# A speech codec's end tiles: another order for the planner's steps, and 89 copies on the other engine

## Chip, cores and metric

The kernel runs on one NeuronCore of a Trainium2 chip. The metric is the time of one execution on the device in microseconds (us). The engines are named as in the profile: PE (TensorE, matrix products, its weight loads as PEld), DVE (VectorE), ACT (ScalarE), POOL (GpSimd) and SP (SyncE, which issues DMAs).

## What is computed

The input x has 2 sequences of 16,000 rows with 512 bf16 values. Each row goes through an encoder, four stages of a residual quantizer with 8 codewords each, and a decoder. The reference, cut:

```python
for i in range(K):                                   # K = 3 taps over rows
    z = z + xp[:, i:i+T, :] * dw_enc[i][None, None, :]
z = _silu(z)
res, q = z, jnp.zeros_like(z)
for s in range(Nq):                                  # 4 stages
    cb = codebooks[s]                                # 8 x 512
    d2 = |res|^2 - 2 res.cb + |cb|^2
    sel = cb[d2.argmin(-1)]
    q, res = q + sel, res - sel
for i in range(K):
    y = y + qp[:, i:i+T, :] * dw_dec[i][None, None, :]
```

The stages depend on each other, since each subtracts the codeword that the one before it chose.

## The kernel before

**Tiles.** Each sequence is cut into nine tiles. A tile has G rows on each of 128 partitions, G = 16 but for the two at the outer ends: the tiles are 4, 10, 16 x 7 and 16 x 7, 10, 4 rows, numbered 0 to 17. The end tiles of four and ten rows make the first and the last stretch of the kernel short.

**Steps of a tile.** The rows are loaded transposed (`XT`, L599, one DMA for each of the G rows, issued by SP). *Front*: for each half of the channels, six products with the taps (L644 on ACT, L645 on DVE), two sums on DVE (L393, `TA` and `ZB`), then exp on ACT (L650), plus one (L651 on ACT, L652 on DVE), reciprocal on ACT (L662), and the gate on DVE (L393, `ZB<-ZB,EX`). Exp and reciprocal lie in different tables, so a change from one to the other costs a table load. *Score*: PE forms products with the codebooks (L674, L681), DVE takes them out (L715, L716). *Decide*: three decisions with short DVE operations (L393, L742, L774); between them PE transposes the one-hot choice (L758), a copy of it (`OT`, L762 on ACT, L763 on DVE) goes back to PE for a correction (L768). The third decision writes `OHD`; PE transposes the one-hots (L791), a copy takes them out (`OHR`, L796, called "win0"). *Resid*: PE rebuilds the residual with the chosen codewords (L838, L843) in four units of 8 and 32 products, and 8 copies write it over `ZB` (L865 on ACT, L866 on DVE). *Score3* and *decide3* choose the fourth codeword on the residual (L881, L882, L890), PE transposes again (L808), a copy takes it out (`OHW`, L814, "win3"). *Back*: PE multiplies the one-hots with the decoder's table (L915, L917, L919), copies to `YB` (L924 on ACT, L925 on DVE), and stores by SP (L952).

**The order.** Nothing is issued at once. Every step is put on a list with its engine, its planned cost and what it depends on: 2408 steps. `Plan.order` then gives out the list. Two strings fix what it does: `RANK` holds two characters for each step, its place in its engine's queue, and `WHERE` holds a letter (A or D) for each of the 608 steps that may run on ACT or on DVE (`either`). Each engine takes its steps strictly by rank. The planner's clock decides only which PSUM bank a product gets and where **filling matmuls** (L973) go: products without a use that are put in front of a PE step when the planner believes that PE would stand idle, so that the granted clock stays up. On the chip each engine runs its queue in order and waits where an operand is not there.

**Buffers around the order.** The residual of tile n+4 shares a `ZB` buffer with tile n: the front of a later tile can write its `ZB` only when the last score of the earlier tile has read it. SP's queue holds loads and stores in one order.

Of the kernel before, what the change touches and what calls it, by code (L numbers as in the profile page):

```python
# [185 lines left out]
def kernel(  # L186
# [31 lines left out]
    NA = 4  # L218
    QUOTA = {"ACT": 4, "DVE": 4}
    DIGITS = "0123456789abcdefghijklmnopqrstuvwxyzABCDEFGHIJKLMNOPQRSTUVWXYZ"  # L220
    RANK = ("00010200010703060F0c070G0e0005010b0k0n0d0i0e0o090J0a0h0j000v03090j060e0405070f0i0u0k0o000D0l0x010202080a0b0e0f0j0k040609"
            "0c0d0g0h0i05060b01040a0407080305090g0l080d02030h0r0y0u0B0v0m0c0Q0V0W0Y1012130q0w0D0g0F0a0b0n0s1p1w1B1l1n1z0c0m0x1q1u1N0n"
            "0j0q0y080d0w0B0C0H0I0L0P0R0f0m0l0C0p0r0U0s0A0t0z0q0h181a1d0O0K0E0T0k1k0o1r0p1s0i1i0M0f0N0g0S0X0Z110p1m14171516191b1c1e0t"
            "0A0z1y0E1A0r1G1H1I1J1L1P1S0l0s0N0t1W1Y202322242627292a0m0u0Q0v2c2e2g2f2h2i2j2k0n0y2m0A0B0T0U0C0D2w2x0E0F0W0Y0G0H0Z0X0J2I"
            "2K2M2N2P0L110N150O3c151j1f1g1h1o1v1t1x0H0J1E0G1C1D1F0I1K1M0K1U0L1Z0O2d0w0z2n0x2o2q2r2s2t2u2v0o0I2B0K2y2z2E2G2H2J2L2O2Q2S"
            "0p0M2X0P2V2W2Y31333435370q0Q170R0S3e190T0U3f1a0V0W3j1e0X0Y1d1c11123q133r3t3u3w3x141i181p1a1q1u191l1b1m1F171k1r040a0b0l0i"
            "0j090c02070d0f08060k030h051T1O1Q1R1V0M1X210R2p252b280P2l0S0V2A102R1232143b0Z103s15163B3D3F3H3J3L3M0r1e3P1g3T3V3X3Z3U3W40"
            "4142430s1i1t1j4447494a4d4e4h4i0t1k4m1l1m1x1A1n1o4t1z1p1q1E1C1r1s1F4A1w1y4P1z1A4U4W4Z51531E1L1I1O23231Z1H1N1K1R1X1L1Q1Z25"
            "2b1G1M2224250A0t0B0z0g0v0o0n0p0m0r0w0x0u0s0q0e0y2T2F2C2D2Z133036181b3a1638393d3h3g3i1f3p1g3y1j3G1d1f3O1c1h3Y4b464g4l4o4s"
            "0u1u1G1x4w4B4D4K4G4H4M4O4Q4S0v1B1J1D4T4X50525456585a0A1J1P1M1N1T1U1O1P1V1W1Q1R1Y1X1U1V202120215J24255Q5S5V5Z6129682c2a2d"  # L230
            "2b2c2b292f2c2o2s2o2t6F2v2l6n2C2u2s0F0H0O0T0S0L0E0N0D0M0R0J0I0Q0C0K0G0P3k3n3l3m3o1h3v3z1n3R3C3K3E3A3N1o3Q3S1u4j1v4q1w4y1v"
            "1C4Y1t1F575d595f5i5k2U5m0w1X5A1Y5p5r5t5y5E5F5G5I5K5L0z2626275M5N5P5U5Y6264660B2a6a2e2g2f2e2h2i2g2h2j2m2j2l2p2q2n2m2y2z6T"
            "2A2F6X6Y74767a2O7j2Q2D2R2G2F2S2E2X7w2M2T2F312N2R2V2H302Q2P120Y0X1316191b181c0Z0U170W10140V111a1s45481r4c4k4f4n1y4z4p4u4r"
            "4v4x1D1B4C1H4N1I551K5c1S1W5D1T285X6560676c6j3I6m0D2n2k2r6o6q6s6t6u6v6x6y6z6A0F2v6D2x6C6E6G6H6I6K6L6O0H2B2r2E2G2w2v2I2J2y"
            "2B2K2M2A7i2N2Y7x2K33347G35377O7T7V7Y823g2U3t363u37343i2X3r34303o333s35383j2Z3p8l2V1j1s1o1v1k1e1t1g1d1m1p1f1l1n1h1q1w1i4F"
            "4J4E4I4L4R4V5b1S5o5e5h5j5g5l5q5n5s1Z5H225O276e2k2o6w2u2w6J6M6N6P6R6S6U0G2D2s2H6V70797c72787e7f7h7l0I2Z2J327r7t7z7C7D7F7H"
            "7J0K362O393a7Z2S3d3e2V2W3h3k32303v3w8E8F3A3E8J3I3L8X8Z9496983Q9c413s3X3u3s3T3l3U3n3k3W3t473y3z3V3m403p3B1B1A1O1x1D1C1G1J"
            "1I1K1H1N1E1L1z1y1M1P5x5w5v5u5z5B5C5R286g5W695T636b6d2d6f2i6p2p6Q2q6W2L2P7m2U2W7v7y7E7I7K7M7N0J382P3f7R7U7X81838587898f8h"
            "0L3m313q8j8m8p8o8r8u8w8x0N3x8C3y3z3b8G3C3D3d3c3F3H3e8S3J3K3f3h3O3P9b3R3S9f9h9n9q9s4a3A4f3G4m3M3N4g3H4l3K3L4n3L4u3O3M4w3R"
            "4q3V411U26281S291V221Y1Q231W1R1T272021240x0y6k6l6i6h6r2t6B6Z2z7p732x7571777d7b7g2C7u2I7B2L7L3b3c8g3l3n8k8t8s8y8z8A8B0M3B"  # L240
            "3a3G8D8H8K8M8L8N8P8Q8R8T0O3M3g3N8U8V92939597999e0P3Y3q44453x3w48499E3B4b4c3D3E4d4e9K3F4o4pad4i4jaeagaiakam4y3S4B3W4C3Y4g"
            "4A3U4P45464L424Z4a4c4V4b554e4h2n2u2j2k2p2h2t2e2d2a2l2g2i2q2r2f0C0E2m7k7n7o7q7s7A2M7P2T8e7S7W7Q2R808684882Y8q388O398I3Z42"
            "9y43469A9C9G9I9L9M9P0Q4h3I4k9R9U9W9Y9Xa0a2a4a5a60R4r3P4va8afajalanaparax0T4D3X4G4H40414N4O44aV4Q4R47b44S4Tb6484W4Ybl5154"
            "bqbubybCbE5e4k5h4o5m4t4B5n4r5z4B4A5K4I5J4K4F5B4C5G4H4D2J2z2w2B2G2L2A2Q2H2K2x2D2C2E2y2I2N2O8a8b8d8c8i8v8n8W3j9l8Y903i919a"
            "3k9d9g3r9t3v9B3z9H4s4tac4x4zatawavaBaDaGaI0S4KaO4MaKaMaPaYaRaXaZb0b3b50U4U494Xb7b9bbbabcbdbebf0W50bj52534d4c56584g4j5b5c"
            "4m4i5k5l4p4q5p5qc45x5ycicncrctcz5L4J5N4L5S4P4I5O4M5R4O4W5U4R5Z4U4S5Y4T604V4N392Z2X3b2T2Y2W333d2U35363a37313c2S329j9i9k3o"
            "9m9o9p9r3C9N9u9w9x9v9z9F9D9J3Ja33Nay3Qaq4F4JaL4E4IaNaTaUb1bgbhbi0V57bp59bkbmbnbvbtbwbAbDbHbI0X5g4l5ibLbQbRbObTbVbXbY105o"
            "c15r5s4uc85t5u4w4x5v5w4z4y5D5E4E4F5M5PcJ5I5QcLcOcQcVcY624W664Z6m594X6k5a6p5c4Z6q5e6w5g506idB6t5d523e3u3w3i3q3n3o3t3p3l3v"
            "3f3m3r3j3h3x3g9O9S9T9Q9V9Za1a73TaAa9abaaahaoasauaz3ZaJ43b246b85a5dbG5f5jbMbUbSc2c3c7c90Y5A4A5CcbcccdcfckcmcocqcvcB0Z5T4Q"
            "5WcGcIcNcTcWcZd1d31261d663644Yd9656750526869dh536c6e57566j6ndL6r6sdTdXdZe1e36ye96O5y6Zf1536E5m6I5p546Q5t6S5z556Keu6V5x56"  # L250
            "3S3I3C3K3U3D3y3R3H3O3G3Q3F3T3J3A3E3PaEaFaHaCaQaSaWbo4hbZbr4fbsbxbzbFbBbJ4nc64sce4vcg5F5Hcw5V5XcRcXcUd2dbdddf116adr6gdidk"
            "dpdtdvdxdAdCdEdF146ldH6odIdKdNdMdOdPdQdS156udV6v6x5k5h6z6A5jee6F6Geo5o6L6M5r5s6T6UeQ6W6YeZf0f5f7f978fg7c5I7vfM5a7j5M7g5N"
            "597ifB7nfD587ofE7p5P57473V4b404a4f3W453Z423Y434d3X49484e44bKbPbNbWc0c5cach4Dcycpclcscjcu4GcxcA4Nd74Sd84Xdg6b6ddo6f6hdudy"
            "dwdDdWe0e4166D5l6He7eaecejeqereteweyez186PeC6ReBeDeIeLeNeOePeR1b6XeW70715Cf87476fa5F777a5Hfn7b7dfq5K7k7lfC7u7zfUfVfYg0g1"
            "7D5U7K5X7M5Y5d7Igi7P5Z5b7G5W7Ogn5c7S6081655e4n4o4p4x4y4w4r4v4l4i4t4m4u4z4q4k4j4scCcDcFcEcHcKcMcP51dld5d4cSd0dadcdedj55dG"
            "58dR5be26B6Ceg6J6NeAeHeJeMeTeUeV1972f375eYfdfifjf6fffkflfmfo1a7e5J7hfpfrfuftfvfyfzfA1d7m5O7q7r5QfJ7s7w5R5S7y7Ag45T7C7F5V"
            "g77J7Ngm7U7YgAgCgDgIgK86gN8a698d6b5f8e6c8i6d5g8fgT8k6e5h8ggU8lgW5i4O4M4T4J4K4G4P4H4L4C4E4Qdndqdm54dsdJdzdU5iehe5e65fdYe8"
            "ebedef5nes5qeF5veX7379fc7ffsfwfxfFfGfHekfI1c7tfL7xfKfNfQfRfPfSfTfWfXfZ1e7Bg37Eg2g6g8g5g9gbgdgg1h7Lgk7Q7R61go7V7X63628083"
            "67668487gP688h8jgV8ogXgYgZh0h18rh38u6j8w6k5k8t6i8vh95j8yhb5l4V4R514U4Y1317eiemenelepevexeE5A5E5ueG5weKeS5Bf2f45Dfb5Gfh5L"
            "fO7Hgagegcgfghgjfegl1f7Tgs7Wgpgqgrgugtgvgwgxgygz1g7Z6482gBgFgGgEgHgJgLgM1i85gO8889gQgR8b8cgS6a8m8n6g6f8p8q6hh28sh4h5h6h7"  # L260
            "h88xha8z6l8A6m5m")
    WHERE = ("DADAAAAADAADDDDADADDDDDDDDDAAADAADDAAAAAADDDDDDDADADDADDDDADADADAAAAAAAAADDDDADDDDDAAADDADAADAAAADAAAAAAAAADDDDADADADDDD"
            "DAAAAAAAAAAADAAAAADDADDDDADDDDDDADDDADAAAAAAAADAAADAAAAADDADDDDDDDAADADAAAAAADDAAAAAAAAADDDDDDDDDDDDDDDAAADAAAAADDDAAAAA"
            "AAADDDDDDDDDDDDADAADADAAADAAAAAAAAAAADDDDADDDADDDDDAAAAADAAADAAAAAAAAAADDDDDADDDDADDDAAAAAADADDAAAAAAAAAADDDDDDDDDADADDD"
            "ADAAAAAAAAAAAAAAAAADDDADDDDDDDDDDDADADAAAAAAAAAAAAADADDDDDDDDDDDDDDAADADAADAAADADAAAADADDDDDDDDADDDDDDDDAAADDAAADADAADDD"
            "ADDDDDDDDDDDADDADDADDAADDAAAADAADAADDDDDDDDDDDDDDDAAADAADAADDAAAADADDDDDADDDDDADDDDDDDADAAAADADAAADDDDDDDDAADADADDDADDDD"
            "AAAADDAA")
    assert B == len(SIZES) and T >= GM * P and GM <= 16

# [83 lines left out]

    plan = Plan(NA, QUOTA, [len(DIGITS) * DIGITS.index(a) + DIGITS.index(b) for a, b in zip(RANK[::2], RANK[1::2])], WHERE)
    add = plan.add
# [655 lines left out]
```

## Time and profile before

| | us |
|---|---|
| three runs | 618.36, 619.06, 619.17 (median 619.06) |
| the profiled execution | 619.28 |
| its span, first to last instruction | 617.2 |
| mean granted clock of PE | 0.976 |
| filling matmuls L973 | 426, busy 106.5 |
| table loads | 36, 1.28 each |

In the profile a line such as `L924 ACT CAST YB<-banks ... x107 | 104.7, 1026 | 16.0 <-PE banks L915 11.8` reads: line, engine, operation, what is written from what, count; total busy us and mean ns of one; idle us of the engine just before them and who ended it. In a timeline the idle time stands in brackets behind the instruction that it precedes, with its releaser. In the chain each piece is start, length and what ran; it is followed back from the last instruction. In a table by stretches each engine has its busy us and, in brackets, its instructions; the last three numbers are the granted clock, the share of the DMA engines and GB/s. Records of neighbouring instructions on one engine overlap by some 0.08 us, so mean and busy time over count differ a little.

### The profile page before, as it was taken

What the parts mean: (1) busy time and instruction counts of PE and PEld (TensorE: products, weight loads), DVE (VectorE), ACT (ScalarE), POOL (GpSimd) and SP (SyncE); (2) the same over time, 40 slices, a digit from 0 to 9 for tenths busy, and PEclk for the clock granted to TensorE, in tenths of its full rate; (3) what the DMA queues carried; (4) which work ended last, traced back from release to release, by engine and by line L of the source; (5) the groups of instructions that cost most, each with busy time, mean ns of one, the idle gap of its engine ahead of it and who ended that gap; (6) DMA issues with size and microseconds to landing.
All of it is one profiled execution on the core that took longest, in us unless ns stands there. A gap on an engine that the chain in (4) does not pass through costs nothing.

```text
span 617.2 us, 27847 instructions
## 1 busy us (share of the span) xinstructions
PE 509.7 (83%) x12649; PEld 244.2 (40%) x12649; DVE 574.7 (93%) x1134; ACT 548.9 (89%) x428; POOL 48.1 (8%) x86
## 2 busy tenths in 40 slices
PE   4797978987877889877895965988988879899995
PEld 3344434433434334343342343444344333434452
DVE  5999999899999999999999999989999999998764
ACT  4899899799999999999969999969999999975563
POOL 1002000110010011011000010101000101000000
PEclk9889999999999999999999987899999999999999
DMA  7424437455637687475575576565646425043236
GB/s 215 95 53 95 83 87 108 82 98 116 107 79 140 125 127 162 87 133 115 126 144 107 118 146 167 115 143 113 89 111 157 128 63 149 4 139 139 83 102 208
DMA packets 155562, 71.84 MB, mean 116 GB/s; under 512 B 146886, under 2 KB 146918, under 8 KB 155316
## 3 DMA queue, kind: packets, MB, share of 16 engines
q1 hardware_dynamic: 155228, 69.64, 52.1%
q8 instruction: 98, 1.61, 1.1%
q10 hardware_dynamic: 216, 0.43, 0.2%
q14 instruction: 20, 0.16, 0.1%
HBM read 2.26 MB, written 32.77 MB: 57 GB/s over the span
## 4 chain that ended last, share of the span: by engine, by line
DVE 48%; PE 18%; ACT 12%; issue 9%; SPq 6%; DMA 5%; ACTq 0%; DVEq 0%
DVE ZB L393 10%; DVE TB L645 7%; DVE TA L393 6%; PE banks L838 5%; DVE TA L645 4%; SPq L599 4%; PE banks L915 3%; DMA XT<-in_x_dram 3%; PE banks L681 3%; PE banks L843 3%; DVE EX L652 3%; ACT TB L644 3%; ACT EX L650 2%; ACT YB L924 2%; ACT ZB L865 2%
## 5 line engine op out<-in xcount | busy, mean ns | idle before, releaser
L924 ACT CAST YB<-banks 128x1024 bf16<-128x1024 f32 x107 | 104.7, 1026 | 16.0 <-PE banks L915 11.8
L865 ACT CAST ZB<-banks 128x1024 bf16<-128x1024 f32 (+2 forms) x107 | 94.3, 925 | 26.1 <-PE banks L843 26.1
L650 ACT ACTIVATE EX<-ZB 128x4096 bf16<-128x4096 bf16 (+2 forms) x36 | 115.3, 3202 | 1.6 <-DVE ZB L393 1.2
L662 ACT ACTIVATE EX<-EX 128x4096 bf16<-128x4096 bf16 (+2 forms) x36 | 114.7, 3193 | 0.5 <-DVE EX L652 0.3
L973 PE MATMUL banks<-MSK,IDENT 128*128 128x512 bf16 x426 | 106.5, 392 | 3.5 <-issue 2.8
L681 PE MATMUL banks<-ZB 128*32 128x64 bf16 x8064 | 92.0, 198 | 5.3 <-DVE ZB L393 3.3
L681 PEld LDWEIGHTS <-ZB 128*32 128x32 bf16 x8064 | 77.3, 96 | 46.6 <-issue 38.7
L915 PE MATMUL banks<-WDEC,OHW 128*128 128x512 bf16 x252 | 73.6, 383 | 18.7 <-ACT ZB L865 4.4
L843 PE MATMUL banks<-OHR,WR 32*128 32x512 bf16 (+3 forms) x1152 | 82.1, 355 | 0.1
L645 DVE TENSOR_SCALAR TB<-XT,WENC 128x2048 bf16<-128x2048 bf16 (+2 forms) x120 | 80.2, 678 | 0.1
L393 DVE TENSOR_TENSOR ZB<-TA,TB 128x4096 bf16<-128x4096 bf16 (+2 forms) x36 | 72.6, 2017 | 5.3 <-PE banks L681 3.4
L838 PE MATMUL banks<-ZB,IDENT 64*64 64x512 bf16 (+3 forms) x576 | 54.9, 369 | 24.2 <-ACT ZB L865 7.2
L393 DVE TENSOR_TENSOR ZB<-ZB,EX 128x4096 bf16<-128x4096 bf16 (+2 forms) x36 | 72.8, 2024 | 1.1 <-ACT EX L662 1.0
L393 DVE TENSOR_TENSOR TA<-TA,TB 128x4096 bf16<-128x4096 bf16 (+2 forms) x36 | 72.5, 2014 | 0.4 <-ACT TB L644 0.3
L753 POOL COPY OHD<-OHA 128x256 bf16<-128x256 bf16 (+2 forms) x36 | 30.6, 850 | 479.5 <-DVE OHA L393 479.5
L973 PEld LDWEIGHTS <-IDENT 128*128 128x128 bf16 x426 | 39.7, 100 | 48.7 <-issue 10.4
L838 PE MATMUL banks<-ZB,UP 64*64 64x512 bf16 (+3 forms) x576 | 53.1, 353 | 0.3 <-issue 0.3
L843 PEld LDWEIGHTS <-WR 32*128 32x128 bf16 x1152 | 23.2, 92 | 59.0 <-issue 51.3
L644 ACT ACTIVATE TB<-XT,WENC 128x2048 bf16<-128x2048 bf16 (+2 forms) x24 | 42.3, 1763 | 2.8 <-DVE ZB L393 2.7
L866 DVE CAST ZB<-banks 128x1024 bf16<-128x1024 f32 (+3 forms) x37 | 38.2, 1042 | 7.0 <-PE banks L843 6.9
L645 DVE TENSOR_SCALAR TA<-XT,WENC 128x2048 bf16<-128x2048 bf16 (+2 forms) x65 | 44.1, 689 | 0.2
L838 PE MATMUL banks<-ZB,DOWN 64*64 64x512 bf16 (+3 forms) x576 | 42.0, 365 | 0.4 <-issue 0.4
(132 smaller groups left out, 602.0 us busy)
## 6 DMA issues: line engine op xcount, KB each, us to landing
out_dram<-YB SPq DMA_DIRECT2D x29, 512.0 KB
out_dram<-YB SPq DMA_DIRECT2D x32, 448.0 KB
XT<-in_x_dram SPq DMA_TRANSPOSE x267
out_dram<-YB SPq DMA_DIRECT2D x28, 60.0 KB
ZB<-in_x_dram SPq DMA_DIRECT2D x1, 1280.0 KB
ZB<-in_x_dram SPq DMA_DIRECT2D x1, 512.0 KB
out_dram<-YB SPq DMA_DIRECT2D x30, 2.0 KB
out_dram<-YB SPq DMA_DIRECT2D x2, 224.0 KB
```

What stands on the lines that cost most here:

```text
L393: add("DVE", cost, key, lambda: nc.vector.tensor_tensor(out=out, in0=a, in1=b, op=op), reads, writes, **kw)
L644: either({"ACT": act(R), "DVE": dve(R, 3.84) + 0.06}, key, lambda dst=dst, src=src, w=w: nc.scalar.mul(dst, src, w), lambda dst=dst, src=s ...
L645: lambda dst=dst, src=src, w=w: nc.vector.tensor_scalar(out=dst, in0=src, scalar1=w, scalar2=None, op0=ALU.mult),
L650: add("ACT", act(2 * R), ("exp", n, h), lambda: nc.scalar.activation(v(ex), Z, ACT.Exp, scale=-1.0), zt, [("EX", sl), "ACTTAB"], hold="E")
L662: nc.scalar.add_instruction(mybir.InstActivation(name=nc.get_next_instruction_name(), engine=mybir.EngineType.Activation, func=ACT.Reciprocal,
L681: nc.tensor.matmul(o[HB * q:HB * (q + 1), u * ZW:(u + 1) * ZW].rearrange("p (s c) -> p s c", s=2), lhsT=blk, rhs=both, start=False, stop=( ...
L838: nc.tensor.matmul(at(r)[to], lhsT=dia[h, h], rhs=Z[h, i, r:G:RG, :], start=start, stop=False)
L843: nc.tensor.matmul(at(r), lhsT=WR[v][g, i * P:(i + 1) * P], rhs=W[g, v // 3, 0:rows_of[r], :], start=False, stop=stop)
L865: either({"ACT": act_psum(2 * k * P), "DVE": dve(2 * k * P)}, key(1), lambda dst=dst, src=src: nc.scalar.copy(dst, src()), lambda dst=dst, ...
L915: nc.tensor.matmul(o, lhsT=W[:, k, PADC:PADC + P], rhs=WDEC[u], start=True, stop=not wrap)
L924: either({"ACT": act_psum(1024), "DVE": dve(1024)}, key, lambda dst=dst, box=box: nc.scalar.copy(dst, ps(box)), lambda dst=dst, box=box: n ...
L973: nc.tensor.matmul(PS[j // 2][:, 512 * (j % 2):512 * (j % 2) + NMK * ZW], lhsT=IDENT, rhs=MSK.rearrange("p u w -> p (u w)"), start=True, s ...
```

## The change

Only the two strings change. No step is added or removed, no cost, buffer or dependency is touched. All lines of `RANK` and all but the last of `WHERE` are new:

```diff
-    RANK = ("00010200010703060F0c070G0e0005010b0k0n0d0i0e0o090J0a0h0j000v03090j060e0405070f0i0u0k0o000D0l0x010202080a0b0e0f0j0k040609"
...
-            "h88xha8z6l8A6m5m")
-    WHERE = ("DADAAAAAADAADDDDADADDDDDDDDDAAADAADDAAAAAADDDDDDDADADDADDDDADADADAAAAAAAAADDDDADDDDDAAADDADAADAAAADAAAAAAAAADDDDADADADDDD"
...
+    RANK = ("00010200010c05080M0d070L0c000j0f0f0k0p0c0g0g0r090N0e0j0t000t050h0m080l0b0k090d070F010r000g0c0B020403040607090a0h0i010208"
...
+            "h38xh58z6q8A6r5m")
+    WHERE = ("DADAAAAADAADADDDADDDDDDDDDAAAADAAADAAAAAADDDDDDDADDDDADDADADADAADAAAAAAAADDDDADDDDDAAADAADAADAAAADDAAAAAAAADDDDADADADDDD"
...
             "AAAADDAA")
```

Read letter by letter against the list of steps, 89 of the 608 steps change engine:

| copies (columns) | ACT to DVE | DVE to ACT |
|---|---|---|
| taps of 16 rows (2048) | 1 (tile 10) | 3 (tiles 6, 9, 13) |
| taps of 10 rows (1280) | 3 | 1 |
| taps of 4 rows (512) | 4 | 3 |
| `OT` (128 and less) | 10 | 7 |
| "win0" `OHR` (1024) | 2 (tiles 8, 15) | 3 (tiles 10, 12, 14) |
| "win3" `OHW` (1024, one of 640) | 1 (tile 2) | 4 (tiles 3, 6, 12, 16) |
| residual (1024) | 10 | 10 |
| residual of end tiles (256 to 768) | 2 | 4 |
| `YB` (1024) | 9 | 11 |
| setup (`WR`, L536) | 0 | 1 |

The queues of PE (533 steps), POOL (81) and SP (333) keep their steps in another order: the longest run of steps that keep their order among themselves is 356, 56 and 131. ACT has 400 steps instead of 395 (253 in the old order), DVE 1061 instead of 1066 (568).

More of the change, by code (lines that the diff above doesn't have):

```diff
@@ L220 @@
     DIGITS = "0123456789abcdefghijklmnopqrstuvwxyzABCDEFGHIJKLMNOPQRSTUVWXYZ"
-    RANK = ("00010200010703060F0c070G0e0005010b0k0n0d0i0e0o090J0a0h0j000v03090j060e0405070f0i0u0k0o000D0l0x010202080a0b0e0f0j0k040609"
[L222 to L260, printed above, removed]
-            "h88xha8z6l8A6m5m")
@@ new lines @@
+    WHERE = ("DADAAAAADAADADDDADDDDDDDDDAAAADAAADAAAAAADDDDDDDADDDDADDADADADAADAAAAAAAADDDDADDDDDAAADAADAADAAAADDAAAAAAAADDDDADADADDDD"
+            "DAAAAAAAAAAAAAAAAADDADDDDADDDDDDADDDDDAAAAAAAADAAADAAAAADDADDDDDDDAADADAAAAAADDAAAAAAAAADDDDDDDDDDDDADDAAAAAAAADDDAAAAAA"
+            "AAADDDDDDDDDDDDADDADAAADAAAAAAAAAAAAADDDDADDDADDDDDDADAADAAAAAAAAAAAAAADDDDDADDDDAADDDAAAADDADAAAAADAAAAADDDDDDDDDADDDDD"
+            "DAAAAAAAAAAAAAAAAAADDDADDDDDDDDDDADDDDAAAAAAAAAAAAADADDDDDDDDDDDDDDDAAADAADAAAAADAAAADADDDDDADDADDDDDDADDAAAADDADAAADAAA"
+            "ADDDDDDDDDDDADDDAADADAADADAADAADAAADDDDDDDDDDDDDDDDDADAAADADDAADDADAADDDDADDDDDDDDDADDAAAADADAADDAAADDDDDDAADDADDDADDDDA"
```

44 lines of the change are left out of this document (39 added, 5 removed).

## Prediction, made before the run

> **What bounds the kernel now.** I read the page first, for the shares.
>
> ```profile
> span 617.2 us, 27847 instructions
> PE 509.7 (83%) x12649; PEld 244.2 (40%) x12649; DVE 574.7 (93%) x1134; ACT 548.9 (89%) x428; POOL 48.1 (8%) x86
> ```
>
> Three engines are above 80%, so a mean says little. I cut the span where the character of the 40 slices changes and asked for the busy time of each engine in three stretches.
>
> ```profile
> 15.00:415.00 400.00, 325.10 (x7693) 155.28 (x7694) 389.61 (x693) 373.42 (x268) 32.65 (x38) 0.97 0.58 114
> 415.00:541.00 126.00, 109.08 (x3067) 51.34 (x3052) 122.99 (x238) 125.17 (x94) 11.12 (x13) 1.00 0.44 101
> 541.00:611.00 70.00, 68.93 (x1854) 31.73 (x1846) 53.81 (x150) 43.10 (x51) 2.45 (x9) 1.00 0.37 130
> ```
>
> The columns are stretch, length, then PE, PEld, DVE, ACT and POOL busy. Up to 541 us DVE idles 10.4 of 400 and 3.0 of 126 us; ACT idles 26.6 and 0.8. So VectorE sets the pace, and from 415 on ScalarE is as full. In the last 70 us PE is busy for 68.9 and the other two are not. The waits of that last stretch (who waited for whom: total us, times, longest) say the same:
>
> ```profile
> ACT ZB L865 <- PE banks L843: 15.3, 11, 3.3
> ACT YB L924 <- PE banks L915: 8.1, 9, 1.5
> DVE ZB L866 <- PE banks L843: 6.6, 8, 1.9
> PE banks L838 <- issue: 0.3, 1, 0.3
> ```
>
> So the time is a sum: the moment at which the decisions of tile 14 are made, which lets PE start that tile's residual, then some 70 us of PE work, then the last copy and store. The hand-over, from the timelines of DVE, PE and ACT, and the end, from the chain:
>
> ```profile
> 537.84 0.28 DVE L393 TENSOR_TENSOR OHD<-KEY,M 128x128 bf16<-128x128 f32 x1
> 539.88 0.68 DVE L796 COPY OHR<-banks 128x1024 bf16<-128x1024 bf16 x1
> ```
>
> ```profile
> 540.60 0.41 PE L838 MATMUL banks<-ZB,IDENT 64*64 64x512 bf16 x4
> ```
>
> ```profile
> 610.37 1.01 ACT YB L924
> ```
>
> The last decision of tile 14 (OHD) ends at 538.12, the copy of its transposed rows (L796) at 540.56, the residual starts at 540.60, the last copies run from 610.37, and the span ends 6.8 us later. The profiled execution took 619.28 us, 2.1 more than its span and 0.2 more than the median of 619.06.
>
> One more thing costs time ahead of the hand-over: **PE trains**. When a tile's third decision is made, PE transposes it, runs four residual products and scores, and both other engines wait for it. From the chain:
>
> ```profile
> 298.95 0.29 DVE OHD L393
> ...
> 314.72 0.66 PE banks L681 x63
> ...
> 315.41 2.29 DVE ZB L393
> ...
> 410.68 0.30 DVE OHD L393
> ...
> 415.60 0.34 PE banks L681 x16
> ...
> 415.96 1.53 DVE ZB L393
> ```
>
> The reader is to see a DVE decision, PE alone, and DVE again: tile 7's train, 299 to 315, and tile 10's, 411 to 416.
>
> **The change part by part.** The 2408 steps are the same ones; the strings only say on which engine a copy runs and where each step stands in its engine's queue. I sorted every queue by the old and by the new ranks and added up, for each step, its duration in this trace (its time beyond the end of the instruction before it).
>
> *Moved copies.* 42 go from ACT to DVE and 47 back. The rates, total over count of these rows (groups by line and shape):
>
> ```profile
> L924 ACT CAST YB<-banks 128x1024 bf16<-128x1024 f32 x107 | 104.7, 1026 | 16.0 <-PE banks L915 11.8 <-PE banks L919 3.9
> L925 DVE CAST YB<-banks 128x1024 bf16<-128x1024 f32 x19 | 22.9, 1216 | 2.8 <-PE banks L915 1.3 <-PE banks L919 1.0 <-issue 0.6
> L644 ACT ACTIVATE TB<-XT,WENC 128x2048 bf16<-128x2048 bf16 x18 | 36.1, 2003 | 2.8 <-DVE ZB L393 2.7
> L645 DVE TENSOR_SCALAR TB<-XT,WENC 128x2048 bf16<-128x2048 bf16 x94 | 69.1, 744 | 0.1
> L814 ACT COPY OHW<-banks 128x1024 bf16<-128x1024 bf16 x8 | 8.2, 1023 | 0.3 <-PE banks L808 0.3
> L796 DVE COPY OHR<-banks 128x1024 bf16<-128x1024 bf16 x8 | 5.4, 680 | 0.0
> ```
>
> Net to ACT go 2 output copies (0.98 us there, 1.21 on DVE), 2 long taps (2.00 and 0.74) and 3 window copies (1.02 and 0.68): ACT +9.0, DVE -5.9. Net to DVE go 3 short taps (two of ten rows, by the long rate times 10/16, one of four rows, by 4/16): ACT -3.0, DVE +1.1. Ten residual copies of 1024 go each way. The rest, net 3 copies of 128 columns to DVE and 5 copies of the end tiles and the setup to ACT, I estimate from the same rates by width: ACT +0.5, DVE -0.7. In all **ACT +6.5, DVE -5.5 us**, over the whole kernel. Table loads stay 36: the order in which exponentials and reciprocals alternate has as many switches.
>
> *Work ahead of the hand-over.* That is what counts. Check of the method: the busy time up to 538.13, grouped, is
>
> ```profile
> 0.00:538.13 538.13, 438.20 (x10719) 210.95 (x10720) 518.34 (x979) 501.68 (x374) 45.29 (x76) 0.97 0.56 114
> ```
>
> and my old queue has 518.3 us of DVE work up to tile 14's decision. In the new one 27 copies worth 16.5 have left, 26 worth 15.0 have come, and a score copy of 0.5 stands behind: 516.4, so **-2.0**. The copy of the rows itself (L796) goes to ACT: +0.3 by the rates. On ACT 26 copies worth 18.9 have left ahead of it and 28 worth 23.6 have come, that copy among them: **+4.7**.
>
> *The train of tile 10.* DVE and ACT idle at it (timelines):
>
> ```profile
> 415.96 2.29 DVE L393 TENSOR_TENSOR ZB<-TA,TB 128x4096 bf16<-128x4096 bf16 x1 [2.20 <-PE banks L681]
> ```
>
> ```profile
> 409.61 1.93 ACT L924 CAST YB<-banks 128x1024 bf16<-128x1024 f32 x2 [2.15 <-PE banks L915]
> 414.94 1.93 ACT L865 CAST ZB<-banks 128x1024 bf16<-128x1024 f32 x2 [3.41 <-PE banks L843]
> 418.33 2.00 ACT L644 ACTIVATE TA<-XT,WENC 128x2048 bf16<-128x2048 bf16 x1 [0.55 <-DVE ZB L393]
> ```
>
> In the new queues decision 10 comes 5.9 us of DVE work earlier, the gate of tile 12 (2.2 us) stands between it and the waiting sum, and on PE the last score of tile 9, which that sum waits for, no longer stands behind the 2.2 us second half of tile 10's first residual product. I take the DVE wait from 2.2 to 0.3: **-1.9**; bounds: 0 (the train waits for ACT) and -2.2. Next late is ACT, which now also copies tile 10's rows.
>
> *ScalarE's way to that copy.* The hand-over is the later of two ways. DVE's stands at -2.0 + 0.3 - 1.9 = -3.6. ACT's is +4.7 less what ACT no longer idles. Between 415 and 541 it has 0.8 us to spare; before, 26.6. The three rows above hold 6.1 of these, and two rows at tile 7's train another 4.3:
>
> ```profile
> 311.19 1.01 ACT L865 CAST ZB<-banks 128x1024 bf16<-128x1024 f32 x1 [1.70 <-PE banks L843]
> 314.76 1.01 ACT L865 CAST ZB<-banks 128x1024 bf16<-128x1024 f32 x1 [2.56 <-PE banks L843]
> ```
>
> Decision 7 comes 3.8 us of DVE work earlier in the new queue, decision 10 5.9. I take the 6.1 and a quarter of the 4.3, 7.2 in all: ACT arrives at 4.7 - 7.2 = **-2.5**, later than DVE, and sets the hand-over. Bounds: +4.7 (nothing absorbed) and -3.6 (DVE's way).
>
> *The last 70 us.* PE has the same 99 steps, 69.3 us, from tile 14's residual to the end in both queues; DVE has 52.6 instead of 54.3 us left, ACT 44.4 instead of 42.6. I take **0**. Bounds: +2 (a dozen order changes among PE's steps, each waiting at most for one copy of 1 us), -1.7 if DVE's share set it.
>
> By the Trainium skill's page Perfetto Trace Analysis (Identifying the Most-Contended Engine), matmul busy time is no measure of how near PE is to its limit, weight loading is; weight loads fill 31.7 of the 70 us, so by that PE has room. The waits quoted above, ACT and DVE for PE and PE for neither, speak against it here. By its rule the last stretch would follow DVE: -1.7, a rival below.
>
> *At nothing.* Two rows of the chain, a burst of filling matmuls and a transposing load on the path:
>
> ```profile
> 105.98 3.73 PE banks L973 x9
> ...
> 369.63 3.37 DMA XT<-in_x_dram
> ```
>
> SP's 333 issues are reordered, loads against stores. Loads that run a tile ahead hide that; one that came late would cost about what the chain shows once, 3.4. POOL keeps its 81 steps in another order, which the other engines' work hides; uncovered, one costs 0.6 (48.1 us over 86 instructions on the page). The filling matmuls (L973) are inserted by the planner and can't be read from the strings: bounds -3.7 (that burst goes) and +3.7 (another comes ahead of a train), taken as 0.
>
> **Sum.** The later of -3.6 and -2.5, and 0 behind it: 619.3 - 2.5 = 616.8 against the profiled execution, **616.6** against the median.
>
> **The rivals.**
> *ScalarE comes late (slower).* The place is tile 14's row copy, now in ACT's queue behind 4.7 us more work. For it: ACT is full from 415 on, and most of its idle time before is waits for PE trains, which more work of its own does not shorten where the train now waits for ACT's copy (tile 10's rows). Against it: decisions come earlier. The time is longer than before by over 1.2 us where ACT absorbs less than 3.5. Price: with nothing absorbed 619.1 + 4.7 = 623.8; with a third of the 4.7 absorbed, the middle of this case, +3: 622.
> *The moves cancel.* DVE reaches its waits earlier and waits longer; the trains set the pace, with their PE work unchanged. For it: PE's work ahead of tile 14's residual is 344.5 us in both queues. 619, within 1.2.
> *DVE sets the last stretch.* Then -1.7 comes on top: 614.9. Against it: the waits.
>
> **How the numbers follow.** Forecast 616.6 (its own range 614.9 to 617.8): 0.38. ScalarE late, 620.3 to 623.8: 0.35. Cancelled, 617.8 to 620.3: 0.17. Below that, 613 to 614.9: DVE setting the last stretch 0.06, the filling burst gone 0.04. A measurement here tells 0.2% (1.2 us) from no change, so faster 0.48, same 0.17, slower 0.35. The range 613.8 to 623.0 leaves out about half of the lowest cases and the top fifth of ScalarE's, some 12 in 100; the filling's and the load's bounds of 3.7 and 3.4 are why it is not cut closer.
>
> **What would show it.** Right: the DVE decision of tile 14 ends near 536 and the residual starts near 538; the sum of tile 13 no longer waits over 0.5 us for PE; PE is busy for 69 of the last 70 us. Wrong: the wait before the residual's first products names ACT's row copy; gates of tiles 9 to 16 wait for reciprocals on ACT; or PE pauses in the last 70 us for copies that ACT now makes. Then the hand-over is later than 540.6 and the time above 620.

## The result, and the profile after

After takes **612.18 us**, the median of three (611.07, 612.18 and 613.92), against 619.06: a ratio of 0.9895 with a 95% interval of 0.9856 to 0.9934. Measured again beside later kernels it took 612.11 against 619.46 (0.9890, 0.9847 to 0.9932). So the direction was right, and the size was not: 616.6 was forecast, and 612.18 lies below the whole range of 613.8 to 623.0.

The profiled execution of after is the slowest of its three, 613.92, 1.7 above the median; that of before was 0.2 above its own. The two traces can show 5.4 of the 6.9 us. The page of after, and its busy times in three stretches (length, then PE, PEld, DVE, ACT and POOL busy):

```profile
span 612.0 us, 27868 instructions
PE 512.3 (84%) x12655; PEld 243.0 (40%) x12655; DVE 570.5 (93%) x1129; ACT 554.5 (91%) x433; POOL 50.4 (8%) x86
```

```profile
15.00:415.00 400.00, 329.69 (x7736) 153.86 (x7734) 390.02 (x694) 381.37 (x272) 36.96 (x38) 0.95 0.58 116
415.00:537.00 122.00, 108.42 (x3015) 51.42 (x3015) 120.69 (x234) 120.82 (x91) 8.68 (x13) 0.99 0.49 99
537.00:606.00 69.00, 67.31 (x1840) 32.18 (x1832) 50.33 (x145) 45.57 (x55) 2.95 (x10) 1.00 0.39 133
```

The picture is the same: VectorE sets the pace up to 415 us, VectorE and ScalarE up to the hand-over, PE behind it (67.3 of 69 us). In all VectorE has 4.2 us less work than before, ScalarE 5.6 more (forecast: 5.5 less, 6.5 more). The waits of the last stretch still name PE:

```profile
ACT ZB L865 <- PE banks L843: 14.6, 10, 2.6
DVE ZB L866 <- PE banks L843: 6.2, 6, 2.5
ACT YB L924 <- PE banks L915: 5.1, 9, 1.2
```

The hand-over of tile 14, from the timelines of VectorE, ScalarE and PE, and the last output copies:

```profile
533.52 0.29 DVE L393 TENSOR_TENSOR OHD<-KEY,M 128x128 bf16<-128x128 f32 x1
```

```profile
534.59 1.02 ACT L924 CAST YB<-banks 128x1024 bf16<-128x1024 f32 x1
535.48 1.04 ACT L796 COPY OHR<-banks 128x1024 bf16<-128x1024 bf16 x1
...
604.84 1.93 ACT L924 CAST YB<-banks 128x1024 bf16<-128x1024 f32 x2 [0.63 <-PE banks L915]
```

```profile
533.87 0.40 PE L791 MATMUL banks<-IDENT,OHD 128*128 128x128 bf16 x4 [0.69 <-DVE OHD L393]
...
534.64 1.22 PE L681 MATMUL banks<-ZB 128*32 128x64 bf16 x128
535.79 0.41 PE L838 MATMUL banks<-ZB,IDENT 64*64 64x512 bf16 x4
...
536.78 0.83 PE L843 MATMUL banks<-OHR,WR 32*128 32x512 bf16 x12
```

The decision ends at 533.81 in place of 538.12 (-4.3), the row copy at 536.52 in place of 540.56 (-4.0), the span at 612.0 in place of 617.2. Behind the row copy 75.4 us are left, 76.6 before: -1.2. The residual's first products (L838) now run while the rows are copied, and only the products with the rows (L843) come behind the copy; in before the first L838 started at 540.60, behind it.

Where the 4 us ahead of the hand-over come from can be read by cutting VectorE's time up to the decision into work and idle time:

```profile
0.00:533.81 533.81, 441.96 (x10666) 208.91 (x10666) 517.01 (x977) 504.97 (x376) 47.39 (x76) 0.96 0.57 115
```

The work is 517.0 us, 518.3 before (-1.3); the idle time is 16.8, 19.8 before (-3.0). These rows of before's VectorE hold the idle time that went:

```profile
10.33 1.47 DVE L590 COPY XT<-banks 128x1024 bf16<-128x1024 bf16 x2 [5.31 <-PE banks L580]
...
116.98 0.42 DVE L715 TENSOR_REDUCE rr<-banks 128x8 f32<-128x256 f32 x1 [1.75 <-PE banks L681]
...
120.31 2.29 DVE L393 TENSOR_TENSOR ZB<-TA,TB 128x4096 bf16<-128x4096 bf16 x1 [0.67 <-ACT TB L644]
```

and these of after's VectorE hold what is left, and what is new:

```profile
10.35 0.69 DVE L590 COPY XT<-banks 128x1024 bf16<-128x1024 bf16 x1 [4.21 <-PE banks L580]
...
354.21 1.42 DVE L645 TENSOR_SCALAR TA<-XT,WENC 128x2048 bf16<-128x2048 bf16 x2 [1.39 <-DMA XT<-in_x_dram]
...
387.13 0.75 DVE L645 TENSOR_SCALAR TB<-XT,WENC 128x2048 bf16<-128x2048 bf16 x1 [2.05 <-DMA XT<-in_x_dram]
...
410.69 2.29 DVE L393 TENSOR_TENSOR ZB<-TA,TB 128x4096 bf16<-128x4096 bf16 x1
```

By tile 1's taps VectorE has idled 7.4 us before and 5.6 after (-1.8, the start). Between 104 and 122 us it idled 2.5, now nothing. The sum of tile 13 behind tile 10's train waited 2.20 and now follows the work ahead of it (410.69 has no wait): -2.2, as forecast. Against that stand two new waits for loads, +1.4 and +2.1. These terms make -3.0, as the row says; the other waits, up to 0.8 us each, cancel. The start, the stretch at 104 to 122 us and the loads, none of them in the forecast's sum, are as large as what was in it.

### The profile page after: what moved, and what is told of

Same layout as the page of the kernel before. It is cut to its first block, busy times and chain, and to the rows that moved or that the text cites. A ratio compares the mean times of both kernels' runs of the same rounds, so it can differ in the third digit from the quotient of the medians.

```text
span 612.0 us, 27868 instructions
## 1 busy us (share of the span) xinstructions
PE 512.3 (84%) x12655; PEld 243.0 (40%) x12655; DVE 570.5 (93%) x1129; ACT 554.5 (91%) x433; POOL 50.4 (8%) x86
## 3 DMA queue, kind: packets, MB, share of 16 engines
q8 instruction: 98, 1.61, 1.1%
## 4 chain that ended last, share of the span: by engine, by line
DVE 17%; PE 15%; SPq 10%; ACT 5%; issue 4%; DMA 3%; ACTq 0%; DVEq 0%
SPq L599 8%; PE banks L838 4%; DVE ZB L393 3%; PE banks L843 3%; PE banks L915 3%; DMA XT<-in_x_dram 3%; DVE TB L645 2%; DVE TA L393 2%; PE banks L681 2%; ACT YB L924 2%; DVE TA L645 2%; DVE ZB L866 1%; ACT ZB L865 1%; SPq L952 1%; DVE EX L652 1%
## 5 line engine op out<-in xcount | busy, mean ns | idle before, releaser
L973 PE MATMUL banks<-MSK,IDENT 128*128 128x512 bf16 x432 | 108.5, 391 | 2.8 <-issue 2.2
L915 PE MATMUL banks<-WDEC,OHW 128*128 128x512 bf16 x252 | 76.5, 401 | 12.4 <-ACT OHW L814 3.8
L843 PE MATMUL banks<-OHR,WR 32*128 32x512 bf16 (+3 forms) x1152 | 83.0, 359 | 0.0
L838 PE MATMUL banks<-ZB,IDENT 64*64 64x512 bf16 (+3 forms) x576 | 55.0, 368 | 19.5 <-ACT ZB L865 5.3
L753 POOL COPY OHD<-OHA 128x256 bf16<-128x256 bf16 (+2 forms) x36 | 33.0, 917 | 432.0 <-DVE OHA L393 428.6
L838 PE MATMUL banks<-ZB,UP 64*64 64x512 bf16 (+3 forms) x576 | 52.9, 354 | 0.0
L644 ACT ACTIVATE TB<-XT,WENC 128x2048 bf16<-128x2048 bf16 (+2 forms) x25 | 44.8, 1801 | 2.9 <-DVE ZB L393 1.6
L843 PEld LDWEIGHTS <-WR 32*128 32x128 bf16 x1152 | 23.4, 92 | 59.3 <-issue 51.6
L838 PE MATMUL banks<-ZB,DOWN 64*64 64x512 bf16 (+3 forms) x576 | 42.3, 368 | 0.0
```

The costliest lines, as they stand in the source:

```text
L838: nc.tensor.matmul(at(r)[to], lhsT=dia[h, h], rhs=Z[h, i, r:G:RG, :], start=start, stop=False)
L843: nc.tensor.matmul(at(r), lhsT=WR[v][g, i * P:(i + 1) * P], rhs=W[g, v // 3, 0:rows_of[r], :], start=False, stop=stop)
L915: nc.tensor.matmul(o, lhsT=W[:, k, PADC:PADC + P], rhs=WDEC[u], start=True, stop=not wrap)
L973: nc.tensor.matmul(PS[j // 2][:, 512 * (j % 2):512 * (j % 2) + NMK * ZW], lhsT=IDENT, rhs=MSK.rearrange("p u w -> p (u w)"), start=True, s ...
```

## The experiments

Every time is the median of several executions, beside that of before in the same series. One execution strays by some us (before's own went from 616.1 to 623.3 in one series), so a single profile shows a mechanism and not a size. The expectations number their theories: 1, the gain is idle time taken out ahead of 126 us; 2, loads in SP's full queue take part of the gain back; 3, pauses of PE decide, by where they fall; 4, the gain is a sum of early leads that are kept; 5, before's later order gives such leads back; 6, it is tile 13's loads that give them back.

| run | us | before | ratio, 95% interval |
|---|---|---|---|
| a: before without one burst of filling matmuls | 618.61 | 618.58 | 1.0009 (0.9987 to 1.0031) |
| b: after with such a burst | 616.94 | 618.58 | 0.9985 (0.9961 to 1.0009) |
| c: new up to 122 us, then old | 617.34 | 618.58 | 0.9981 (0.9954 to 1.0008) |
| d: old up to 126 us, then new | 622.92 | 618.58 | 1.0070 (1.0046 to 1.0094) |
| e: after again | 612.11 | 619.46 | 0.9890 (0.9847 to 0.9932) |
| f: after without small stores | 610.63 | 619.46 | 0.9852 (0.9824 to 0.9879) |
| g: before without small stores | 618.15 | 619.46 | 0.9984 (0.9963 to 1.0005) |
| h: after with SP in old order | 625.39 | 619.46 | 1.0085 (1.0058 to 1.0112) |
| i: after, small stores by POOL | 614.98 | 619.35 | 0.9937 (0.9914 to 0.9959) |
| j: after, 9 filling matmuls fewer | 610.75 | 619.35 | 0.9875 (0.9844 to 0.9905) |
| k: after, 20 fewer | 611.85 | 619.35 | 0.9888 (0.9863 to 0.9912) |
| l: new up to 40 us, then old | 619.68 | 619.35 | 1.0006 (0.9992 to 1.0020) |
| m: new up to 300 us, own fills | 617.61 | 619.49 | 0.9959 (0.9937 to 0.9982) |
| n: new up to 430 us, own fills | 613.80 | 619.49 | 0.9909 (0.9885 to 0.9933) |
| o: d with own fills | 616.94 | 619.49 | 0.9970 (0.9942 to 0.9998) |
| p: i for tiles 0 to 10 alone | 610.97 | 619.49 | 0.9865 (0.9836 to 0.9893) |
| q: c with p's stores | 618.62 | 619.85 | 0.9985 (0.9959 to 1.0012) |
| s: j and p together | 611.64 | 619.85 | 0.9859 (0.9836 to 0.9881) |

**The burst at 106 us (a, b).** The stall at 104 to 122 us looked like the filling matmuls' doing. In before's timelines of PE and ScalarE:

```profile
105.98 3.73 PE L973 MATMUL banks<-MSK,IDENT 128*128 128x512 bf16 x9 [2.45 <-issue]
```

```profile
110.45 3.00 ACT L924 CAST YB<-banks 128x1024 bf16<-128x1024 f32 x3 [2.86 <-PE banks L919]
```

PE pauses 2.45 us, then spends 3.73 us on fills, and the output products that ScalarE waits for stand behind them. Run a leaves these fills out of before, b puts nine into after:

```diff
-            if s["fill"]:
+            if s["fill"] and s["n"] != 352:
```
```diff
+            if s["n"] == 342:
+                fill(s["spare"], 9)
```

(`s["spare"]` is the bank that the planner would fill.)

> Before, with the 9 filling matmuls left out that stand at 105.98 us ahead of tile 1's output products (they compute nothing of the output). In before ScalarE waits 2.86 us for the products behind that burst, and VectorE 1.75 and 0.67 us behind ScalarE. Theory (most of the gain is idle time taken out ahead of 126 us and carried to the end): 616.2 to 616.8, 2.4 to 2.9 less than before. Rival 1 (an early lead is given back at later waits, and the gain is made behind 126 us): 618.5 to 619.5. Rival 2 (PE's pause of 2.45 us ahead of the burst, which waits for nothing that the profile shows, is the cause, not the burst): the pause lasts longer in the place of the burst, and the time is 618 or more.

> After, with 9 more filling matmuls (they compute nothing of the output) put ahead of tile 1's output products of the first row pair, near 104 us, some 3.7 us of PE at the rate of before's burst. Theory: ScalarE's three output copies at 105.3 wait about 2.5 us again, VectorE behind it, and nothing later gives it back: 614.4 to 615.2, 2.2 to 3 more than after. Rival 1 (an early delay is absorbed later): 612 to 612.8.

Run a gives nothing, 618.61 against 618.58. Its ScalarE and VectorE show why:

```profile
123.29 2.00 ACT L644 ACTIVATE TB<-XT,WENC 128x2048 bf16<-128x2048 bf16 x1 [3.94 <-DMA XT<-in_x_dram]
```

```profile
128.29 0.29 DVE L736 TENSOR_TENSOR PR<-banks,S 128x128 bf16<-128x128 f32 x1 [2.90 <-PE banks L768]
```

The stall went, VectorE stood 2.4 us ahead at tile 4's taps, and within 10 us the lead was gone: ScalarE waited 3.94 us for a transposing load of tile 5, and the chain behind it took VectorE's 2.90. So before's order takes an early lead back, and the theory of idle time ahead of 126 us, as a cause by itself, falls with a.

In b the nine fills cost some 5 us (616.94 against after's 612.1), more than their own 3.7, and ScalarE waits 1.47 us for those products where after has no wait. But b's trace does not show that the early delay lasts: tile 10's decision ends at 405.93, in after at 406.13. Of the 2.7 us by which b's span is longer, 0.8 lie ahead of tile 14's decision and 1.9 behind it, where PE pauses 0.73 and 1.66 us without a visible cause (timeline of PE):

```profile
603.35 1.02 PE L915 MATMUL banks<-WDEC,OHW 128*128 128x512 bf16 x4 [1.66 <-issue]
```

The last section comes back to such pauses. What the early delay itself costs in after's order is not shown.

**Half the change (c, d, l).** A step's engine and its place come from one version up to a cut in time, from the other behind it:

```
queue[e] = [n for n in first[e] if start[n] < cut] + [n for n in second[e] if not start[n] < cut]
```

> The order and the engines of after for the steps that start ahead of 122 us in after's trace, those of before for all others; the filling matmuls follow the planner's rule. VectorE's lead of after over before at that place is 4.5 to 5.0 us. Theory: 614.2 to 615, about 4.5 less than before. Rival 1 (the gain is made behind): 617 or more. A seam that costs something would raise both.

> The order and the engines of before for the steps that start ahead of 126 us in before's trace, those of after for all others; the filling matmuls follow the planner's rule. Theory: only what the change gives behind that point is left, 2 to 2.5 us: 616.5 to 617.2. Rival 1 (the gain is made behind): 614 or less.

> The order and the engines of after for the steps that start ahead of 40 us in after's trace, those of before for all others; filling matmuls by the planner's rule. After's VectorE stands 1.6 us ahead there, for want of 1.9 us of idle time at the start. Theory 1 (an early lead is kept): 617 to 618. Rival (before's later order gives it back, as it did with the burst): 618.3 to 620.

Early alone gives 1.2 us (c, its interval includes zero), the new start alone nothing (l), late alone is slower by 4.3 (d). The parts do not add up to 7. But d and l carry something of their own in the last stretch, where the planner's rule put six and four fills (before has two there, after one) and PE pauses once for about 2 us. PE in d:

```profile
608.70 0.81 PE L973 MATMUL banks<-MSK,IDENT 128*128 128x512 bf16 x3 [2.27 <-issue]
```

From tile 14's decision to the end d takes 82.6 us and l 81.5, where before takes 79.0 and after 78.2. Their times do not answer the question, and cuts were made again (m, n, o); l, the new start, was not.

**SP's queue (e to h).** Run a pointed to the loads. SP issues them one behind the other, most of them 1.3 to 1.8 us each, between the output stores. In before nine issues, the last of tile 13's loads and the first of tile 14's, take 12.84 us without a gap (timeline of SP):

```profile
380.02 12.84 SPq L599 DMA_TRANSPOSE XT<-in_x_dram  x9
```

Runs f and g leave the small output stores out (those rows are not written), h gives after before's order on SP alone:

```diff
-        for p0, p1, lo, hi in parts:
+        for p0, p1, lo, hi in [r for r in parts if r[1] - r[0] >= 16]:
```

> After, unchanged, in the same call as the next three, so that they are compared with it. 611 to 613.5 if the first measurement holds (612.18).

> After without the small output stores: the 58 store DMAs of fewer than 16 partitions (60 KB and 2 KB each) are left out, so those output rows are not written. Only SP's queue gets shorter, by some 0.55 us for each, about 32 us over the kernel, and with it the transposing loads that stand behind stores come earlier. Theory 2 (loads in SP's queue pace the first 430 us beside VectorE: after loses 1.4 us at 351 and 2.1 us at 385 to loads that come late, and the run without the burst lost its gain to one): 2.5 to 3.5 us less than after. Theory 1 (idle time ahead of 126 us, nothing else): within 1 us of after. If the pauses of PE at every 128th matmul set the rest, also within 1 us.

> Before without the same 58 small stores (those output rows are not written). Theory 2: VectorE waits for no load in before's trace beyond 0.4 us, so at most 1 us less than before, 617.5 to 619. If the loads pace before too through their effect on ScalarE and on what VectorE is given to do, 2 to 4 us less: 614.5 to 616.5.

> After with SP's queue in before's order; all other queues as in after, filling matmuls by the planner's rule (462 in place of 432). Theory 2: the order of the loads against the stores is part of the gain, and the time goes back by 2 us or more, to 614 or above. Theory 1: SP's order is worth nothing, 611.5 to 613.

In f the waits for loads at 354 and 387 us, 1.4 and 2.1, shrink to 0.4 and 0.3, and tile 14's decision comes at 530.0 in the profile, but the median falls by 1.5 us only, less than the 2.5 to 3.5 expected and with an interval that overlaps after's; g gains 1.3, with an interval that includes zero. Run h was the surprise: with SP's old order the new order loses 13.3 us and is slower than before. Its VectorE waits for tile 13's loads, and later for a store that frees an output buffer:

```profile
388.02 0.75 DVE L645 TENSOR_SCALAR TB<-XT,WENC 128x2048 bf16<-128x2048 bf16 x1 [1.48 <-DMA XT<-in_x_dram]
```

```profile
525.54 1.22 DVE L925 CAST YB<-banks 128x1024 bf16<-128x1024 f32 x1 [2.84 <-DMA out_dram<-YB]
```

Part of the 13 us is again fills, eight in the last stretch, which lasts 82.3 us from the decision on; the decision itself comes 5.2 us later than in after. What follows: SP's order is no free choice; it fits one order of the other queues.

**POOL and a shift of PE's stream (i, j, k).** Run i issues the small stores from POOL; j and k take 9 and 20 of 28 fills out of a burst at 117 us, behind which PE idles in any case.

```diff
+            queue = nc.sync if p1 - p0 >= 16 else nc.gpsimd
+            queue.dma_start(out=view[p0:p1, lo:hi, :], in_=Y[p0:p1, lo - g0:hi - g0, :])
```
```diff
+                j, k = s["fill"]
+                fill(j, k - 9 if s["n"] == 424 else k)
```

> After, with the 58 small output stores (fewer than 16 partitions) issued by POOL in place of SP; nothing is left out. Theory 2 (SP's queue, full with transposing loads up to 430 us, gives back part of the gain at 351 and 385): as with those stores left out, 610 to 611.5, so 0.5 to 2 us less than after's 612.1. Rival: POOL, which is in order, holds its copies of decisions back while it waits for a store's rows, and the trains wait for it: 613 or more.

> After, with 19 filling matmuls in place of 28 in the burst at 117 us, at whose end PE idles 0.97 us for VectorE's decision (they compute nothing of the output). It takes no work off the path; it only shifts all later matmuls by 9 places against the multiples of 128 at which PE's pauses without a visible cause fall. Theory 3 (where these pauses fall makes microseconds; it is why the run with 9 more ended 80.1 us behind the hand-over and not 78.2): another time than 612.1 by over 1 us, more likely longer, with other pauses in the trace. Rival: the pauses are hidden, 611.5 to 612.7.

> After, with 8 filling matmuls in place of 28 in the same burst: a shift by 20 places. Theory 3: a time of its own, over 1 us from 612.1 or from the shift by 9. Rival: 611.5 to 612.7. If the granted clock falls because PE is filled less, the time is longer and the clock in the slices after 117 us shows it.

In i tile 14's decision comes at 530.7, earlier than in after (533.8, 532.8 in e), but 9.5 us pass from PE's last product to the end of the span, 6.5 in after, and the time is 614.98: the rival's number, but not its reason, since the trains come earlier. The shifts give 610.75 and 611.85, 1.4 and 0.3 us from after, with intervals that overlap after's. The pauses move to other times; j is over 1 us from after, as theory 3 asked, but not clear of noise. Theory 3 as the main cause of some 7 us falls.

**The cuts again (m, n, o).** The filling matmuls are fixed by a table: each step keeps the number that it has in before or in after, according to its side of the cut.

```diff
-            if s["fill"]:
-                fill(*s["fill"])
+            if s["n"] in FILLS:
+                fill(s["spare"], FILLS[s["n"]])
```

> The order and the engines of after for the steps that start ahead of 300 us in after's trace, those of before for all others. Each step keeps the filling matmuls that it has in after or in before, so that none is added. VectorE's lead there is 5 to 7 us. Theory 4 (the gain is a sum of leads of VectorE, most of them made ahead of 300 us, and kept): 613.5 to 615.5. Theory 5 (before's later order gives an early lead back, only the whole order gains): 617 or more.

> The same with the cut at 430 us, so that the trains of tiles 7 to 10 and their loads stand in the new order too; the last tiles and the last 70 us stand in before's. Theory 4: 612 to 614. Theory 5 with the end as its part: 616 or more. The difference to the cut at 300 is what the stretch of the trains and of the late loads is worth: by theory 4 0.5 to 2 us (2.2 less at tile 10's train, up to 3.7 more at loads).

> The order and the engines of before for the steps that start ahead of 126 us in before's trace, those of after for all others, as in the run of before (622.9), but each step keeps its own filling matmuls, so that the four in the last stretch are gone. Theory 4: 616.5 to 618.5, what the change gives behind 126 us. Theory 5: 619 or more, the late part does not gain without the early one.

Run o has d's queues and only other fills (431 in place of 445), and takes 616.94 in place of 622.92: 6 us from filling matmuls alone, by what they take and by how they shift PE's stream. The cuts now line up: new up to 300 us gives 1.9 us, up to 430 us 5.7, the whole 7.4 (e); new behind 126 us alone (o) gives 2.5. So half of the gain, 3.8 us, comes only when the stretch from 300 to 430 us is moved as well. The 1.7 behind it are within the spread of e. Theory 4 named the size for n and o and was wrong on m.

What happens in that stretch is read from VectorE's lead over before. In m it is 7.6 us at tile 7's decision, 3.0 behind its train, where the seam lies, and 1.2 at tile 10's decision; in n it is 7.8, 6.9 and 7.5. The first loss of m may be in part the seam's own: at this train m's VectorE waits 2.42 us for a reciprocal of ScalarE, where before waits 0.78 and after 0.45. The second loss of m is a load:

```profile
388.10 0.75 DVE L645 TENSOR_SCALAR TB<-XT,WENC 128x2048 bf16<-128x2048 bf16 x1 [1.73 <-issue]
```

The profile names no releaser here, but beside VectorE's own work this instruction needs only tile 13's loads, the last of which was issued up to 385.0. Of the kernels with before's order on SP here, c, m and h wait in the same way and start these taps at 388.5, 388.1 and 388.0; before itself comes at 389.3 and does not wait. In c, which has no seam near, the lead shrinks there from 2.6 to 0.8 us. With the new order on SP the taps start behind such a wait at 387.1 (after), 385.2 (e) and 384.5 (n). **Tile 13's loads are a gate**, in before's order near 388 us, and 25 us later tile 10's train is a second one. It is no fixed time: in the program a load of tile 13 waits for the taps of tile 11, and SP's queue moves with the rest. In a, which has before's order on SP too, the last of these loads was issued 3 us later than in m, and the taps waited until 391.1; in o, with after's order here but late, until 390.7.

**Both gates (p, q, s).** Run p is i with POOL's stores for tiles 0 to 10 alone (`st["n"] < 11`), q puts the same into c, s into j.

> After, with the small output stores of tiles 0 to 10 issued by POOL, the later ones by SP as in after; nothing is left out. With all of them on POOL tile 14's decision came 2 to 3 us earlier than in after, but the last rows landed 3 us later. Theory 2 (SP's queue gives back part of the gain): 609 to 610.5. Rival (what SP gives is lost behind the hand-over in any case): 612 or more.

> The run with the new order up to 122 us (617.3, 1.2 less than before beside it), with the small output stores of tiles 0 to 10 issued by POOL. Theory 6 (tile 13's loads, in SP's full queue, give the early lead back): VectorE's first taps of tile 13 start ahead of 387 us without a wait for a load, and the time is 614.5 to 616.3; what is left of the lead is cut by the wait at tile 10's train, 2.2 us, which before's order keeps. Rival (something else gives it back): 617 or more.

> After with the small output stores of tiles 0 to 10 issued by POOL (611.0 alone) and with 19 in place of 28 filling matmuls in the burst at 117 us (610.75 alone). If the two add up: 609 to 610. If both take the same idle time: 610.5 to 611.5.

In q's trace the first gate is open: VectorE keeps a lead of 4.0 us to tile 10's decision, without a wait for tile 13's loads. At the train behind it the lead shrinks to 2.7, because the wait of 2.20 us grows:

```profile
413.24 2.29 DVE L393 TENSOR_TENSOR ZB<-TA,TB 128x4096 bf16<-128x4096 bf16 x1 [3.49 <-PE banks L681]
```

The time did not fall (618.62 against 619.85, the same ratio as c within its interval), so what the trace shows of the gates is not confirmed by the clock in this kernel. Run p takes 610.97, 1.1 less than after, and s 611.64: the two edits do not add up, and none of j, p and s is shown to beat after at this spread. All three beat before.

The copies alone, on their new engines in the old order, were not tried, nor was the new order with the copies on their old engines: with either mix the planner comes to a point where no engine's next step can start. How much of the gain is the copies' is open.

## Why the prediction was wrong, step by step

*Time as hand-over plus last stretch.* Right: 4.0 of the 5.2 us of span lie ahead of the row copy's end, 1.2 behind it.

*Work ahead of the hand-over, -2.0.* About right: -1.3 in after's trace. In the second one:

```profile
0.00:532.83 532.83, 425.35 (x10583) 206.50 (x10666) 516.45 (x977) 504.77 (x376) 47.78 (x76) 0.97 0.58 115
```

516.45 is -1.9; the decision ends there at 532.83, 5.3 us earlier than in before.

*The train of tile 10, -1.9.* Right, -2.2. By the traces of q and m it is also a gate, at which an early lead shrinks; that fits the new order giving 1.9 us up to 300 us and 5.7 up to 430 us, which holds this train and tile 13's loads together.

*ScalarE sets the hand-over, at -2.5.* The mechanism is right, the size is not, and **this is the step that failed**. The transposed rows were ready at 534.27, and ScalarE took them at 535.48, behind an output copy. Up to the copy's end ScalarE's time is

```profile
0.00:536.52 536.52, 444.54 (x10815) 210.68 (x10815) 519.69 (x983) 507.68 (x379) 47.39 (x76) 0.96 0.56 115
```

in after, and in before

```profile
0.00:540.56 540.56, 440.30 (x10794) 212.17 (x10794) 520.42 (x985) 504.11 (x377) 45.69 (x77) 0.97 0.55 114
```

So it had 3.6 us more work (forecast 4.7) and 7.6 us less idle time, 28.8 in place of 36.5 (forecast 7.2): -4.0 where -2.5 was forecast; in e, whose copy ends at 535.63, -4.9. That 7.6 is near 7.2 is luck, for the idle time went at other places. The forecast took 6.1 us at tile 10's train and 1.1 at tile 7's. At tile 10's train after's ScalarE still waits 4.2 (5.8 in e):

```profile
401.75 1.93 ACT L865 CAST ZB<-banks 128x1024 bf16<-128x1024 f32 x2 [0.89 <-PE banks L843]
413.07 2.00 ACT L644 ACTIVATE TA<-XT,WENC 128x2048 bf16<-128x2048 bf16 x1 [3.28 <-DVE ZB L393]
```

The second is the tap that waited 0.55 in before. At tile 7's train the two rows of 4.3 are one of 1.66. Most of the rest went ahead of the trains, above all at the stall of 104 to 122 us, where before's ScalarE waited 2.86 and 0.55 and after's 0.61. In the sum this term and the last 70 us, taken as 0 and measured as -1.2, make the 2.7 us by which the trace lies below the forecast.

*VectorE's way, -3.6; and "at nothing".* The decision came 4.3 us earlier (5.3 in e), where the forecast's -2.0 and -1.9 make 3.9. So this way is near in size, again with other contents. The sum held one wait and set the start, the loads and the filling matmuls at nothing; in the traces VectorE's idle time ahead of the hand-over also lost 1.8 at the start and 2.5 at 104 to 122 us, and gained 3.4 at the loads of two tiles, as much as the bound set for one late load. Run a shows that such a lead is worth nothing in before's order, and m and n that it is kept once the loads and the trains between 300 and 430 us are moved too. SP's order, set at nothing because "loads that run a tile ahead hide that", decides 13 us when it is put back alone (h, part of it fills), and filling matmuls decide 6 (d against o).

*The last 70 us, 0.* -1.2, within the bound of -1.7. What was seen is that the residual's first products no longer stand behind the row copy, and that a pause of PE without a visible cause, 0.42 us at 608.7, stands in before's last stretch and none in after's. That the order of this stretch makes the rest is not shown: from the decision to the end it takes 78.2 and 78.7 us in a and m, with before's order, and 77.8, 78.2, 78.3 and 79.7 in p, after, e and o, with after's, all six without such a pause. The rule of the Trainium skill's page Perfetto Trace Analysis (Identifying the Most-Contended Engine), that matmul busy time is no measure and weight loading is, made a rival of -1.7 by VectorE's share; the size is near it, but the trace does not agree with its reason: weight loads fill 32.2 of the 69 us, PE is busy for 67.3, and the long waits are still for PE.

*What the traces leave open.* The two traces show 5.2 us of span, e's 6.0, where the medians show 6.9 and 7.4. Some 1.5 us are read from no trace.

*The rivals.* ScalarE was not late: it absorbed the work. The moves did not cancel, but run a is that rival at work in before's order. The range ended at 613.8 because its lower end took in single causes, the last stretch or a burst; that several terms at nothing could go the same way was not in it.

## What to carry to other kernels

A wait that goes in one place gains only what the next gate lets through, so list the gates behind it (a queue of loads that is full, a train that all wait for) and ask which of them the change moves as well; where it moves all of them, add up the early waits, and do not set them at nothing. When two schedules are spliced for a test, freeze whatever a rule would insert anew, or the test measures the rule.

## What the runs showed of the chip

PE pauses at one place in its stream: behind the first 30 us, all its pauses above 0.3 us that wait for nothing visible, five in before and seven in after, stand behind 95 matmuls of a block of 128, so that the next one is number 96 of its block. The count is the one behind PE's busy time in a window that ends in the pause, here two of before (105.98 and 119.21, the second of 0.41 us) and two of after (1.22 us at 264.98 and 1.09 at 412.61):

```profile
0.00:105.90 105.90, 82.04 (x1375) 43.05 (x1376) 97.49 (x229) 91.99 (x87) 7.33 (x32) 0.97 0.50 103
0.00:119.20 119.20, 94.62 (x1631) 49.20 (x1632) 108.96 (x249) 102.33 (x93) 9.64 (x33) 0.96 0.51 105
```

```profile
0.00:264.90 264.90, 216.07 (x4703) 104.31 (x4704) 256.04 (x502) 246.37 (x190) 24.89 (x50) 0.97 0.55 112
...
0.00:412.50 412.50, 334.22 (x7775) 158.77 (x7776) 396.98 (x746) 385.41 (x288) 38.81 (x64) 0.95 0.58 118
```

1375, 1631, 4703 and 7775 are 10, 12, 36 and 60 times 128, plus 95. In m, n, o, p, q and s, whose traces also hold all matmuls, all 42 such pauses stand at this place. Most blocks pass without a pause. The planner of both kernels reckons with such blocks: it has `CHUNK, FIRST, FETCH = 128, 33, 4.2` and starts its count at 33, so that its first block ends behind 95 matmuls. A matmul is two instructions here, a weight load and a product, so a block is 256. The Trainium skill's page Runtime: NRT & Kernel Launch (Instruction fetch mechanics) says that instructions are refilled in blocks of 16 KiB, 256 instructions, and that this is mostly hidden. The trace agrees with the size: before's row of the instruction queue has 98 packets and 1.61 MB, 16.4 KB each, and 12649 matmuls are 98.8 blocks.

```profile
q8 instruction: 98, 1.61, 1.1%
```

It is not hidden where 128 short products go by in 1.3 us, as just ahead of before's pause of 2.45 us:

```profile
102.20 1.33 PE L681 MATMUL banks<-ZB 128*32 128x64 bf16 x128
```

The blocks ahead of the pauses in before and after took PE 1.3 to 4.4 us, and the two quickest of before's 99 are among them. That the pauses are instruction fetches is argued from place and size; no run changes the fetch itself.

In the last stretch, where PE sets the pace, such pauses go with a longer time. From tile 14's decision to the end it is 77.8 to 78.7 us in after, a, e, m and p, which have none there (o, without one too, has 79.7), and 79.5 in c, 80.0 in b, 81.5 in l, 82.3 in h and 82.6 in d, which have 1.9 to 2.6 us of them; l, h and d have four to eight fills there as well, so the share of each is open. (f, g and i, which store otherwise, are left out.) Nine filling matmuls far ahead are enough to move a pause there, as b shows.
